# One load of 128 rows in place of loads of 112 and of six rows

## The chip, the cores and the metric

The kernel runs on one core of a Trainium2 chip. The metric is device time in microseconds (us), the median of several executions. Five engines work side by side: TensorE (PE; its weight loads are PEld), VectorE (DVE), ScalarE (ACT), GpSimd (POOL) and SyncE (SP), which here issues nearly all DMAs. Sixteen DMA engines move the data.

## The reference

A causal dynamic convolution over seven tokens feeds a soft mixture of experts, and that feeds a mixture of experts with one expert per token.

```python
# x [4, 3584, 192], weight_gen [4, 3584, 8, 7], float32
w = softmax(weight_gen, axis=-1)              # seven taps a token and head
x_pad = concat([zeros((B, 6, D)), x], axis=1)
out[b, s, h, :] = sum(w[b, s, h, k] * x_pad[b, s + k, h, :] for k in range(7))
x = out.reshape(14336, 192)
# soft MoE: logits = x @ phi (32 slots); dispatch softmax over tokens gives slot inputs,
# eight expert MLPs of four slots each, combine softmax over slots gives tokens
# second MoE: the gate's best expert of eight for each token, scaled by two gates
```

## The kernel before, in words

The convolution is done as matrix products with a banded matrix. A sequence of 3,584 tokens is cut into 32 runs of `BT` = 112 outputs. The matrix of one run and one head has 112 columns (the outputs) and `BI` = 118 rows (the inputs: six tokens in front, and the 112 themselves), with seven diagonals of taps. `band` (L316) makes it, for eight heads at once, on VectorE or GpSimd: it multiplies a tile of taps by a 0/1 mask. `conv` (L330) multiplies it with x on TensorE (L336), head by head.

A block `g` (there are `NG` = 32) holds two batches and two runs of outputs; a pair of blocks `m` holds all four batches. `load_x(g)` (L294) brings the x rows of a block into one of three buffers, `load_v(m)` (L277) the taps of a pair of blocks into one of two buffers `vt`. The taps come from `vscr` in DRAM: their softmax is made in six pieces on VectorE, GpSimd and ScalarE (L150 to L207), turned so that a diagonal becomes a column, and stored there by `w_store` (L209). `vscr` has K - 1 = 6 rows in front of each sequence, which a store of zeros fills (L596).

The 118 rows are brought by two loads for each run `q`: one of 112 rows (L305 for x, L280 for taps) and one of the last six (L307 and L282). So a block issues four x loads, and a pair of blocks four tap loads. The first run of a sequence has no tokens in front; GpSimd writes zeros there (L299).

The main loop over `g` (from L648) issues in this order: `load_x(g + 2)`, on odd blocks `load_v` two pairs ahead, the copies out of the block before, the bands of block g + 1, the convolution of block g in between, scores and the dispatch softmax of the pairs before, and at its end one load of expert weights for the soft MoE (`load_moe(g - 1)`: L268, L270 and L272, 512, 256 and 768 KB in turn, for blocks 1 to 24). All of these loads go through SyncE's one queue in the order of the program, as do the loads (L146) and stores (L212) of the tap pieces. A load of x waits until the convolution that last read its buffer is over, a load of taps until its bands are made and its `vscr` rows are stored. The order of the steps is written out by hand (`PRO`, `PS`, `CS`). After the 32 blocks come the slot MLP, the gate, and the second MoE, which writes the output; they are not touched.

Of the kernel before, what the change touches and what calls it, by code (L numbers as in the profile page):

```python
# [9 lines left out]
F32 = mybir.dt.float32  # L10
# [4 lines left out]
ALU = mybir.AluOpType  # L15
# [43 lines left out]
def dram_ap(t, off, dims):  # L59
    return bass.AP(t.tensor, t.offset + off, [list(d) for d in dims])  # L60
# [3 lines left out]
def attn_moe_moe_kernel(ctx: ExitStack, tc: tile.TileContext, x, wgen, phi, mw1, mw2, w_gate, w_ogate, w1, w2, out, dbg=None):  # L64
    nc = tc.nc
    P = 128
    B, S, D = x.shape
    H, K = wgen.shape[2], wgen.shape[3]
    GR = D // H
    HK = H * K  # L70
# [1 line left out]
    E, _, F = mw1.shape  # L72
    N = B * S
    BT = 112
    BI = BT + K - 1
    MT = 2 * BT
    NM = S // MT
    NG = 2 * NM
    RH = 28 + K - 1
    FC = F // P  # L80
    NT = N // P
    SROW = S + K - 1
    HC = D // 2
    CW = 4 * MT
    NC = S // CW
# [2 lines left out]
    xf = x.rearrange("b s d -> (b s) d")  # L88
# [6 lines left out]
    cpool = pool(ctx, "cpool", 1)  # L95
    dpool = ctx.enter_context(tc.tile_pool(name="dpool", bufs=1, space=DRAM))
    vscr = dpool.tile([B, SROW, HK], F32, tag="vscr", name="vscr")
    cscr = dpool.tile([2, NS, N], F16, tag="cscr", name="cscr")
# [30 lines left out]
    def w_load(i):  # L129
        rt, t0 = RTS[i], T0S[i]  # L130
        rh = rt + K - 1

        e = wg01[:, i * rh : (i + 1) * rh] if i < 2 else pw.tile([P, RH, H, K], F32, tag="wg", name=f"wg_{i}", bufs=2)
        ef = e.rearrange("p t h k -> p (t h k)")
        off = t0 * HK
        last = t0 + 32 * rt == S
        if last:
            nc.gpsimd.memset(ef[:, rt * HK : rh * HK], 0.0)

            for a, z in ((0, 16), (16, 31)):  # L140
                nc.sync.dma_start(
                    ef[B * a : B * z, rt * HK : rh * HK],
                    dram_ap(wf, off + (a + 1) * rt * HK, [[rt * HK, z - a], [S * HK, B], [1, (K - 1) * HK]]),
                )
        n = rt if last else rh
        nc.sync.dma_start(ef[:, 0 : n * HK], dram_ap(wf, off, [[rt * HK, 32], [S * HK, B], [1, n * HK]]))  # L146
        pcs[i] = [e, None, None, None]
# [61 lines left out]
    def w_store(i):  # L209
        rt, t0 = RTS[i], T0S[i]  # L210
        vr = pcs.pop(i)[2].rearrange("p t h k -> p (t h k)")
        nc.sync.dma_start(dram_ap(vscr, (t0 + K - 1) * HK, [[rt * HK, 32], [SROW * HK, B], [1, rt * HK]]), vr[:, 0 : rt * HK])  # L212

    wg01 = pw.tile([P, RH, H, K], F32, tag="wg", name="wg_01", bufs=2)
    w_load(0)
    zrow = cpool.tile([K - 1, HK], F32, tag="zrow", name="zrow")
    nc.gpsimd.memset(zrow, 0.0)
    w_load(1)
    warmup = cpool.tile([K - 1, 1], F32, tag="warmup", name="warmup")
    nc.scalar.activation(warmup, zrow[:, 0:1], AF.Exp)  # L220


# [1 line left out]
    make_identity(nc, ident)  # L224
    mask_s = cpool.tile([BI, BT], F32, tag="mask_s", name="mask_s")
    nc.gpsimd.memset(mask_s, 1.0)

    nc.gpsimd.affine_select(mask_s, mask_s, pattern=[[-1, BT]], compare_op=ALU.is_ge, fill=0.0, base=0, channel_multiplier=1)
    nc.gpsimd.affine_select(mask_s, mask_s, pattern=[[1, BT]], compare_op=ALU.is_ge, fill=0.0, base=K - 1, channel_multiplier=-1)
    phi_p = cpool.tile([P, 2, NS], F32, tag="phi_p", name="phi_p")  # L230
    nc.gpsimd.memset(phi_p, 0.0)
    ones1 = cpool.tile([P, P], F16, tag="ones1", name="ones1")
# [12 lines left out]
    vbank = pt.tile([P, 512], F32, tag="mask", name="vbank", bufs=1)  # L245
    mask = vbank[0:BI, 0:BT]

# [29 lines left out]
    def load_v(m):  # L277
        vt = p2.tile([BI, B, 2, HK], F32, tag="vt", name=f"vt_{m}")
        for q in range(2):
            nc.sync.dma_start(vt[0:BT, :, q, :], dram_ap(vscr, (m * MT + q * BT) * HK, [[HK, BT], [SROW * HK, B], [1, HK]]))  # L280
        for q in range(2):
            nc.sync.dma_start(vt[BT:BI, :, q, :], dram_ap(vscr, (m * MT + (q + 1) * BT) * HK, [[HK, K - 1], [SROW * HK, B], [1, HK]]))  # L282
        vts[m] = vt


# [3 lines left out]

    xbuf = [px.tile([BI, 4 * D + 8], F32, tag=f"x4{i}", name=f"x4_{i}") for i in range(3)]  # L290
    for t in xbuf:
        nc.gpsimd.memset(t[:, 4 * D : 4 * D + 8], 0.0)

    def load_x(g):  # L294
        m, hf = divmod(g, 2)
        t = xbuf[g % 3]
        if m == 0:
            for bb in range(2):
                nc.gpsimd.memset(t[0 : K - 1, 2 * bb * D : (2 * bb + 1) * D], 0.0)  # L299
        r0 = 2 * hf * S + m * MT - (K - 1)  # L300
        v = t[:, 0 : 4 * D].rearrange("p (b q d) -> p b q d", b=2, d=D)
        h = K - 1
        for q in range(2):
            a = h if m == 0 and q == 0 else 0
            nc.sync.dma_start(v[a : a + BT, :, q, :], dram_ap(xf, (r0 + q * BT + a) * D, [[D, BT], [S * D, 2], [1, D]]))  # L305
        for q in range(m == 0, 2):
            nc.sync.dma_start(v[BT:BI, :, q, :], dram_ap(xf, (r0 + (q + 1) * BT) * D, [[D, h], [S * D, 2], [1, D]]))  # L307
        xts[g] = t


# [254 lines left out]
    h = RH // 2  # L565
    for i, st in PS.items():
        ops = [
            (w_load, i), (w_max, i, 0, h), (w_max, i, h), (w_sub, i, nc.gpsimd, 0, h), (w_sub, i, nc.gpsimd, h), (w_exp, i, 0, h), (w_exp, i, h),
            (w_red, i, 0, h), (w_red, i, h), (w_add, i, 0, h), (w_add, i, h), (w_rec, i, 0, h), (w_rec, i, h), (w_rot, i, range(0, 3)), (w_rot, i, range(3, K)),
        ]  # L570
        for t, (f, *a) in zip(st, ops):
            if t >= 0:
                at_step(t, f, *a)
        at_step(st[-1], w_store, i)
# [7 lines left out]
    for g in range(3):  # L582
        load_x(g)
# [9 lines left out]
    w_rot(0, range(0, 6))  # L593
    w_rot(0, range(6, K), nc.gpsimd)
    w_store(0)
    nc.scalar.dma_start(dram_ap(vscr, 0, [[HK, K - 1], [SROW * HK, B], [1, HK]]), zrow.unsqueeze(1).to_broadcast([K - 1, B, HK]))  # L596
    load_v(0)

    def warm_up():
# [4 lines left out]
    def store_1():  # L604
        w_store(1)
        load_phi(4, H)
        load_v(1)
        w_load(3)
# [39 lines left out]
    for g in range(NG):  # L648
        m, hf = divmod(g, 2)
        run = g < NG  # L650
        if 2 < g + 2 < NG:
            load_x(g + 2)
        if run and hf == 1 and m + 2 < NM:
            load_v(m + 2)
# [97 lines left out]
    for i in range(2):  # L752
        r, v = slice(64 * i, 64 * i + 64), slice(16 * i, 16 * i + 16)
# [557 lines left out]
    for f in range(2):  # L1311
        a, z = 4 * f, 4 * f + 4
# [50 lines left out]
    for g in range(NGR):  # L1363
        hi, lo = hh.pop(g)
        ot = f2.tile([P, 4, D], F32, tag="ot", name=f"ot_{g}", bufs=3)
        for j in range(4):
            if j == HJ and g + 2 < NGR:
                hidden(Gm, g + 2, 0, 1)
            t = 4 * g + j
# [57 lines left out]
```

## Time and profile before

| | us |
|---|---|
| median of 3 executions | 281.48 |
| lowest, highest | 281.1, 283.66 |
| the profiled execution | 284.04 |
| its span, first to last instruction | 282.3 |
| TensorE, VectorE busy | 222.2, 228.4 |
| GpSimd, ScalarE busy | 151.0, 148.0 |

The profile is of one execution of its own, and its rows add up to its own span. A group of rows below says which view it is; a wait is put down to what ended it last. "PEclk" is the share of TensorE's full clock that was granted, "DMA share" the mean busy share of the 16 DMA engines.

### The profile page before, as it was taken

How to read it: one execution, taken by the hardware profiler on the slowest of the kernel's cores; microseconds unless marked ns; L12 is line 12 of the kernel's file. 1: busy time of each engine (PE TensorE's matmuls, PEld its weight loads, DVE VectorE, ACT ScalarE, POOL GpSimd, SP SyncE). 2: the span in 40 equal slices, each digit the busy share in tenths (PEclk: the TensorE clock that was granted, in tenths of full speed). 3: DMA queues.
4: the chain of work that ended last, by engine and by line, in shares of the span. 5: the costliest groups of instructions: out<-in, count | busy, mean ns of one | idle time of the engine just before them, and what ended most of it. 6: DMA issues, size and time to landing. Idle time of an engine off the chain costs nothing.

```text
span 282.3 us, 9568 instructions
## 1 busy us (share of the span) xinstructions
PE 222.2 (79%) x3844; PEld 164.2 (58%) x3844; DVE 228.4 (81%) x469; ACT 148.0 (52%) x349; POOL 151.0 (53%) x143
## 2 busy tenths in 40 slices
PE   0017299587986997998969979999878899989980
PEld 0016166365654675776647656754656688878970
DVE  2999999956699399899986998477868797788980
ACT  3102166334653366654574757735405496969970
POOL 6285698785486299658974697325401122314000
PEclk9999989998898699999999999999995999999996
DMA  6625287779699879979998963238579246578773
GB/s 208 160 61 172 92 226 207 231 225 263 177 233 278 240 190 241 262 157 242 295 233 202 228 162 106 63 80 188 128 200 243 49 147 192 179 229 266 233 229 112
DMA packets 63256, 53.82 MB, mean 191 GB/s; under 512 B 19649, under 2 KB 59685, under 8 KB 63205
## 3 DMA queue, kind: packets, MB, share of 16 engines
q1 hardware_dynamic: 63175, 53.14, 69.9%
q8 instruction: 32, 0.52, 0.9%
q14 instruction: 19, 0.16, 0.2%
q10 hardware_dynamic: 30, 0.01, 0.0%
HBM read 37.07 MB, written 16.06 MB: 188 GB/s over the span
## 4 chain that ended last, share of the span: by engine, by line
PE 43%; DVE 19%; DMA 18%; ACT 6%; issue 5%; SPq 1%; POOL 1%; ACTq 0%; DVEq 0%; POOLq 0%
DMA x<-in_x_dram 11%; PE tp L365 8%; PE psA L336 7%; DVE bt L322 5%; PE psB L336 5%; PE L L351 4%; DMA out_dram<-ot 3%; PE op L1372 3%; PE sp L430 2%; PE op L1375 2%; PE op L1374 2%; PE op L1373 2%; DMA vt<-vscr 2%; DMA w1t<-in_moe_w_dram 2%; PE hp L1064 2%
## 5 line engine op out<-in xcount | busy, mean ns | idle before, releaser
L322 POOL TENSOR_TENSOR bt<-vt,mask_s 118x896 f32<-118x896 f32 x51 | 101.5, 2015 | 39.4 <-PE psB L336 19.4
L322 DVE TENSOR_TENSOR bt<-vt,vbank 118x896 f32<-118x896 f32 x77 | 80.0, 1079 | 3.6 <-PE psB L336 2.3
L336 PE MATMUL psA<-bt,x 118*32 118x112 f32 x1024 | 53.7, 279 | 29.2 <-issue 11.2
L369 ACT ACTIVATE at<-tp 112x384 f32<-112x384 f32 x62 | 30.2, 490 | 54.2 <-PE tp L365 53.8
L336 PE MATMUL psB<-bt,x 118*32 118x112 f32 x1024 | 53.6, 272 | 0.5 <-DMA x<-in_x_dram 0.2
L336 PEld LDWEIGHTS psA<-bt,x 118*32 118x32 f32 x1024 | 25.5, 113 | 47.2 <-issue 23.9
L365 PE MATMUL tp<-ident,aT 128*112 128x128 f32 x256 | 44.1, 293 | 0.7
L365 PEld LDWEIGHTS tp<-ident,aT 128*112 128x112 f32 x256 | 26.9, 137 | 17.1 <-issue 12.8
L336 PEld LDWEIGHTS psB<-bt,x 118*32 118x32 f32 x1024 | 33.3, 116 | 1.7 <-issue 0.9
L1377 ACT ACTIVATE ot<-op,S 128x192 f32<-128x192 f32 x77 | 29.4, 437 | 5.9 <-DMA out_dram<-ot 3.1
L1372 PE MATMUL op<-wm,hi 128*128 128x192 f16 x112 | 27.5, 245 | 3.7 <-DVE ot L1379 2.0
L1375 PE MATMUL op<-Ml,cT 128*128 128x192 f16 x112 | 27.5, 246 | 0.2 <-DVE Ml L1296 0.2
L1373 PE MATMUL op<-wm,lo 128*128 128x192 f16 x112 | 27.5, 245 | 0.1
L1374 PE MATMUL op<-wm,hi 128*128 128x192 f16 x112 | 27.5, 246 | 0.1
L1066 DVE SCALAR_TENSOR_TENSOR lo<-hp,hi 128x512 f16<-128x512 f32 x28 | 19.1, 681 | 3.6 <-ACT hi L1065 3.6
L166 ACT ACTIVATE wg<-wg 128x952 f32<-128x952 f32 (+3 forms) x11 | 9.0, 828 | 21.0 <-DVE wg L162 9.1
L351 PE MATMUL L<-aT,phi_p 128*32 128x224 f32 x256 | 19.3, 395 | 0.0
L1065 ACT ACTIVATE hi<-hp 128x512 f16<-128x512 f32 x28 | 16.9, 605 | 3.6 <-PE hp L1064 3.3
L344 ACT ACTIVATE aT<-psA 128x448 f32<-128x448 f32 x31 | 16.7, 539 | 3.2 <-PE psA L336 3.2
L162 POOL TENSOR_TENSOR wg<-wg,mx 128x952 f32<-128x952 f32 (+3 forms) x9 | 14.1, 1573 | 7.2 <-DVE mx L155 7.2
L344 ACT ACTIVATE aT<-psB 128x448 f32<-128x448 f32 x31 | 17.0, 548 | 0.0
L1379 DVE TENSOR_SCALAR ot<-op,S 128x192 f32<-128x192 f32 x35 | 13.7, 410 | 3.0 <-DMA out_dram<-ot 2.9
(259 smaller groups left out, 388.4 us busy)
## 6 DMA issues: line engine op xcount, KB each, us to landing
x<-in_x_dram SPq DMA_DIRECT2D x64, 168.0 KB
w2s<-in_moe_w_dram SPq DMA_DIRECT2D x8, 768.0 KB
out_dram<-ot SPq DMA_DIRECT2D x15, 384.0 KB
w1a<-in_moe_w_dram SPq DMA_DIRECT2D x8, 512.0 KB
cT<-cscr SPq DMA_DIRECT2D x8, 448.0 KB
vt<-vscr SPq DMA_DIRECT2D x32, 98.0 KB
out_dram<-ot SPq DMA_DIRECT2D x9, 288.0 KB
vscr<-vr SPq DMA_DIRECT2D x3, 784.0 KB
```

The costliest lines, as they stand in the source:

```text
L322: (nc.gpsimd if onp else nc.vector).tensor_tensor(bt.rearrange("p h (r k) -> p h r k", k=K), vt.unsqueeze(2).to_broadcast([BI, H, BT // K, ...
L336: nc.tensor.matmul(pss[g][h // 4][r : r + 32, q, :], xt[:, q * D + GR * h : q * D + GR * h + 32], bt[:, h, :], start=True, stop=True, tile ...
L344: nc.scalar.activation(aT[:, c, :], ps.rearrange("p q t -> p (q t)"), AF.Copy)
L351: nc.tensor.matmul(Ls[m][32 * b : 32 * b + 32, :], phi_p[:, c, :], aTs[2 * m + b // 2][:, c, (b % 2) * MT : (b % 2 + 1) * MT], start=(c == ...
L365: nc.tensor.transpose(tp[:, q, c, :], aTs[g][:, c, o : o + BT], ident)
L369: nc.scalar.activation(o, i, AF.Copy)
L1066: low = lambda: nc.vector.scalar_tensor_tensor(lo[:, f, :], hp, 0.0, hi[:, f, :], op0=ALU.max, op1=ALU.subtract)
L1372: nc.tensor.matmul(op, hi[:, 0, tok], wm2[:, 0, :], start=True, stop=False)
L1373: nc.tensor.matmul(op, lo[:, 0, tok], wm2[:, 0, :], start=False, stop=False)
L1374: nc.tensor.matmul(op, hi[:, 0, tok], wm2[:, 1, :], start=False, stop=False)
L1375: nc.tensor.matmul(op, cT[:, t * P : (t + 1) * P], Ml, start=False, stop=True)
L1377: nc.scalar.activation(ot[:, j, :], op, AF.Copy, scale=S0[:, t : t + 1])
```

## The change

A run's input has 128 rows (`BI = P`): 16 tokens in front of the outputs (`PAD = P - BT`) and the 112 themselves. The mask keeps the seven diagonals, ten rows lower, and the added ten rows of the banded matrix are zeros. `vscr` gets 16 rows in front of each sequence, the store of zeros and the memsets of x cover 16 rows, and each run's rows come in one load: two loads a block for x, two a pair of blocks for the taps.

```diff
--- before.py
+++ after.py
@@ -72,14 +72,15 @@
     E, _, F = mw1.shape
     N = B * S
     BT = 112
-    BI = BT + K - 1
+    PAD = P - BT
+    BI = P
     MT = 2 * BT
     NM = S // MT
     NG = 2 * NM
     RH = 28 + K - 1
     FC = F // P
     NT = N // P
-    SROW = S + K - 1
+    SROW = S + PAD
     HC = D // 2
     CW = 4 * MT
     NC = S // CW
@@ -209,14 +210,14 @@
     def w_store(i):
         rt, t0 = RTS[i], T0S[i]
         vr = pcs.pop(i)[2].rearrange("p t h k -> p (t h k)")
-        nc.sync.dma_start(dram_ap(vscr, (t0 + K - 1) * HK, [[rt * HK, 32], [SROW * HK, B], [1, rt * HK]]), vr[:, 0 : rt * HK])
+        nc.sync.dma_start(dram_ap(vscr, (t0 + PAD) * HK, [[rt * HK, 32], [SROW * HK, B], [1, rt * HK]]), vr[:, 0 : rt * HK])
 
     wg01 = pw.tile([P, RH, H, K], F32, tag="wg", name="wg_01", bufs=2)
     w_load(0)
-    zrow = cpool.tile([K - 1, HK], F32, tag="zrow", name="zrow")
+    zrow = cpool.tile([PAD, HK], F32, tag="zrow", name="zrow")
     nc.gpsimd.memset(zrow, 0.0)
     w_load(1)
-    warmup = cpool.tile([K - 1, 1], F32, tag="warmup", name="warmup")
+    warmup = cpool.tile([PAD, 1], F32, tag="warmup", name="warmup")
     nc.scalar.activation(warmup, zrow[:, 0:1], AF.Exp)
 
 
@@ -225,8 +226,8 @@
     mask_s = cpool.tile([BI, BT], F32, tag="mask_s", name="mask_s")
     nc.gpsimd.memset(mask_s, 1.0)
 
-    nc.gpsimd.affine_select(mask_s, mask_s, pattern=[[-1, BT]], compare_op=ALU.is_ge, fill=0.0, base=0, channel_multiplier=1)
-    nc.gpsimd.affine_select(mask_s, mask_s, pattern=[[1, BT]], compare_op=ALU.is_ge, fill=0.0, base=K - 1, channel_multiplier=-1)
+    nc.gpsimd.affine_select(mask_s, mask_s, pattern=[[-1, BT]], compare_op=ALU.is_ge, fill=0.0, base=K - 1 - PAD, channel_multiplier=1)
+    nc.gpsimd.affine_select(mask_s, mask_s, pattern=[[1, BT]], compare_op=ALU.is_ge, fill=0.0, base=PAD, channel_multiplier=-1)
     phi_p = cpool.tile([P, 2, NS], F32, tag="phi_p", name="phi_p")
     nc.gpsimd.memset(phi_p, 0.0)
     ones1 = cpool.tile([P, P], F16, tag="ones1", name="ones1")
@@ -277,9 +278,7 @@
     def load_v(m):
         vt = p2.tile([BI, B, 2, HK], F32, tag="vt", name=f"vt_{m}")
         for q in range(2):
-            nc.sync.dma_start(vt[0:BT, :, q, :], dram_ap(vscr, (m * MT + q * BT) * HK, [[HK, BT], [SROW * HK, B], [1, HK]]))
-        for q in range(2):
-            nc.sync.dma_start(vt[BT:BI, :, q, :], dram_ap(vscr, (m * MT + (q + 1) * BT) * HK, [[HK, K - 1], [SROW * HK, B], [1, HK]]))
+            nc.sync.dma_start(vt[:, :, q, :], dram_ap(vscr, (m * MT + q * BT) * HK, [[HK, BI], [SROW * HK, B], [1, HK]]))
         vts[m] = vt
 
 
@@ -296,15 +295,12 @@
         t = xbuf[g % 3]
         if m == 0:
             for bb in range(2):
-                nc.gpsimd.memset(t[0 : K - 1, 2 * bb * D : (2 * bb + 1) * D], 0.0)
-        r0 = 2 * hf * S + m * MT - (K - 1)
+                nc.gpsimd.memset(t[0:PAD, 2 * bb * D : (2 * bb + 1) * D], 0.0)
+        r0 = 2 * hf * S + m * MT - PAD
         v = t[:, 0 : 4 * D].rearrange("p (b q d) -> p b q d", b=2, d=D)
-        h = K - 1
         for q in range(2):
-            a = h if m == 0 and q == 0 else 0
-            nc.sync.dma_start(v[a : a + BT, :, q, :], dram_ap(xf, (r0 + q * BT + a) * D, [[D, BT], [S * D, 2], [1, D]]))
-        for q in range(m == 0, 2):
-            nc.sync.dma_start(v[BT:BI, :, q, :], dram_ap(xf, (r0 + (q + 1) * BT) * D, [[D, h], [S * D, 2], [1, D]]))
+            a = PAD if m == 0 and q == 0 else 0
+            nc.sync.dma_start(v[a:BI, :, q, :], dram_ap(xf, (r0 + q * BT + a) * D, [[D, BI - a], [S * D, 2], [1, D]]))
         xts[g] = t
 
 
@@ -593,7 +589,7 @@
     w_rot(0, range(0, 6))
     w_rot(0, range(6, K), nc.gpsimd)
     w_store(0)
-    nc.scalar.dma_start(dram_ap(vscr, 0, [[HK, K - 1], [SROW * HK, B], [1, HK]]), zrow.unsqueeze(1).to_broadcast([K - 1, B, HK]))
+    nc.scalar.dma_start(dram_ap(vscr, 0, [[HK, PAD], [SROW * HK, B], [1, HK]]), zrow.unsqueeze(1).to_broadcast([PAD, B, HK]))
     load_v(0)
 
     def warm_up():
```

## Rows read from the trace of the kernel before

**Rows 1.** Windows: length, busy PE, PEld, DVE, ACT, POOL, PEclk, DMA share, GB/s

```profile
45.00:60.00 15.00, 11.39 (x230) 7.73 (x222) 13.90 (x27) 6.16 (x16) 11.50 (x7) 1.00 0.83 237
60.00:80.00 20.00, 17.00 (x335) 11.56 (x333) 13.71 (x19) 10.81 (x24) 13.33 (x8) 0.91 0.85 200
80.00:100.00 20.00, 16.45 (x300) 11.51 (x302) 15.48 (x31) 8.13 (x21) 11.42 (x7) 0.83 0.94 257
100.00:120.00 20.00, 17.95 (x406) 12.92 (x402) 17.92 (x25) 12.90 (x30) 17.30 (x10) 1.00 0.89 227
120.00:140.00 20.00, 18.80 (x395) 12.81 (x388) 19.79 (x38) 10.08 (x26) 15.25 (x10) 1.00 0.89 237
```

**Rows 2.** TensorE's waits, 45:100, 100:140, 140:170 us: total, times, longest

```profile
PE psA L336 <- DMA x<-in_x_dram: 7.0, 3, 2.6
...
PE psA L336 <- DMA x<-in_x_dram: 2.6, 3, 1.6
...
PE psA L336 <- DMA x<-in_x_dram: 1.4, 1, 1.4
```

**Rows 3.** Lines L307, L282: issue ns min/median/max; who waited (us, times)

```profile
L307 SPq DMA_DIRECT2D x<-in_x_dram x62: 272/290/443, 4.0 to 172.3; - x62
...
  PE psA L336: 11.0, 7
...
L282 SPq DMA_DIRECT2D vt<-vscr x32: 263/340/896, 14.8 to 168.0; - x32
...
  POOL bt L322: 8.8, 2
```

**Rows 4.** SyncE's issues in order of time from 63.8 us: start, us, issue

```profile
63.86 0.40 SPq L272 DMA_DIRECT2D w2s<-in_moe_w_dram  x1
64.35 2.28 SPq L305 DMA_DIRECT2D x<-in_x_dram  x2
66.68 0.69 SPq L307 DMA_DIRECT2D x<-in_x_dram  x2
67.98 0.85 SPq L280 DMA_DIRECT2D vt<-vscr  x2
68.88 3.24 SPq L282 DMA_DIRECT2D vt<-vscr  x2
...
72.77 0.32 SPq L305 DMA_DIRECT2D x<-in_x_dram  x1
```

**Rows 5.** Waits of SyncE's queue, 30 to 170 us: total, times, longest

```profile
SPq L282 <- DMA w2s<-in_moe_w_dram: 7.7, 4, 2.2
...
SPq L282 <- DMA wg<-in_weight_gen_dram: 4.0, 1, 4.0
SPq L282 <- DMA w1a<-in_moe_w_dram: 3.9, 4, 1.3
```

**Rows 6.** A window at 90 us; matmuls on x in it; all of L336

```profile
90.00:94.30 4.30, 4.21 (x56) 2.90 (x58) 2.69 (x3) 0.00 (x0) 0.00 (x0) 0.50 0.75 187
...
L336 PE MATMUL psA<-bt,x x16: 363/394/396, 90.1 to 91.0; 118*32 118x112 f32 x16
...
L336 PE MATMUL psA<-bt,x x1024: 256/259/397, 22.7 to 181.8; 118*32 118x112 f32 x171
```

**Rows 7.** The page's DMA packets and main queue

```profile
DMA packets 63256, 53.82 MB, mean 191 GB/s; under 512 B 19649, under 2 KB 59685, under 8 KB 63205
...
q1 hardware_dynamic: 63175, 53.14, 69.9%
```

**Rows 8.** Matmuls of L430 and L351; two groups of VectorE

```profile
L430 PE MATMUL sp<-at,d x256: 324/327/352, 48.3 to 186.7; 112*32 112x193 f32 x128
...
L351 PE MATMUL L<-aT,phi_p x256: 350/353/581, 36.7 to 183.3; 128*32 128x224 f32 x128
...
L322 DVE TENSOR_TENSOR bt<-vt,vbank 118x896 f32<-118x896 f32 x77 | 80.0, 1079 | 3.6 <-PE psB L336 2.3 <-DMA vt<-vscr 0.7
...
L513 DVE TENSOR_REDUCE cmx<-T 128x28 f32<-128x896 f32 x4 | 4.3, 1079 | 0.2
```

## The prediction

> **What bounds the kernel now.** I read the windows first, then TensorE's waits, then who issued what those waits were for. The change touches loads and tiles of the attention stage alone (convolution, scores and slot sums of 32 blocks, matmuls from 22.7 to 181.8 us of the span [rows 6]).
>
> In the windows [rows 1] no single engine is full between 45 and 100 us: TensorE is busy 44.8 of 55 us, VectorE 43.1, and the DMA engines run at 0.83, 0.85 and 0.94. From 100 to 140 us VectorE is nearly full (17.92 and 19.79 of 20 us). So until 100 us something makes three busy parties wait for each other, and after it VectorE sets the pace.
>
> TensorE's own waits name it [rows 2]. From 45 us on it stands 7.0 us for x until 100 us, 2.6 us until 140 and 1.4 us until 170: 11.0 us. The reader should note which x load these are. The view of the six-row load [rows 3] lists these seven waits, 11.0 us, under L307: that is the last of a block's loads to be issued, and the last to land. The six-row tap load L282 in the same way holds GpSimd for 8.8 us.
>
> Why are these late? SyncE's queue shows it [rows 4]. It issues in program order. From the w2s load at 63.86 us count on: two and two x loads, two tap loads, then the two six-row tap loads, which take 3.24 us together though one issue is 0.34 us at the median [rows 3]. The second is the eighth DMA after w2s, and the waits of the queue [rows 5] say that L282 stood for a landing of w2s 7.7 us in four waits, for wg 4.0 us, for w1a 3.9 us. So eight DMAs may be under way, each new one takes the place of the one eight before it, and in this order the second L282 always takes the place of a big weight load. Behind it stand a weight load and the next block's x load (72.77 us), and meanwhile the DMA engines run dry.
>
> **The change, part by part.** *Fewer issues.* 62 six-row x loads (0.290 us at the median) and 32 tap loads (0.340 us) go: 18.0 + 10.9 = 28.9 us of SyncE's time [rows 3].
>
> *The order of eight.* Two blocks now issue 14 DMAs (4 + 4 of x, 2 + 2 of taps, 2 of weights); after it 8 (4, 2, 2). Each DMA then takes the place of its own counterpart two blocks earlier, unless a load or store of the tap weights lies between. A pair of blocks lasts 10 us on the mean (159 us for 16), and the w2s load above landed some 8 us after its issue, so the stands of rows 5, 15.6 us, should end or shrink to the slowest landings. What is late next: an x load still waits until its buffer is free (the convolution of three blocks before), which leaves it two blocks' time, and for the tap store that waits on VectorE.
>
> *What of TensorE's wait that frees.* Three things cap it, by stage. From 45 to 100 us: the waits are 7.0 us; VectorE's idle time 55 - 43.1 = 11.9 us; the DMA engines' idle time 0.17 x 15 + 0.15 x 20 + 0.06 x 20 = 6.75 us. DMA is the tightest. Less the added traffic of this stretch (1.3 us, below) it leaves 5.5 us. From 100 to 140 us VectorE has 2.3 us idle against 2.6 us of waits; as it already sets the pace there, I take 1.0. From 140 to 170 us the one wait of 1.4 us follows the same kind of stand; I take 1.0. Sum 7.5 us.
>
> *TensorE's clock.* It was granted 0.91 and 0.83 in the windows from 60 to 100 us [rows 1], which at the half level of 1.2 GHz is (0.09 + 0.17) x 20 / 0.5 = 10.4 us. In the stretch from 90.0 us, right behind a 2.6 us wait [rows 2], it was 0.50 [rows 6], and a convolution matmul took 394 ns there against 259. If the waits go, so may these, for up to 10.4 x (1 - 259 / 394) = 3.6 us. The sum is capped by DMA, so I leave this out and keep it for the low end.
>
> *Added traffic.* A block's x rows go from 472 packets of 768 B to 512 (the first two blocks: 20 more each), the taps of a pair of blocks from 944 of 224 B to 1,024: 1,240 + 1,280 packets and 40 of the zero store, 1.25 MB. The queue's row [rows 7] gives 0.699 x 16 x 282.3 = 3,157 us of engine time for 53.14 MB in 63,175 packets: 59.4 us a MB, 50 ns a packet. By bytes the added packets cost 74 us of engine time, 4.6 us on 16 engines; by count 128 us, 8.0 us. They are smaller than the mean of 841 B, so bytes are nearer: 4.6 us over 32 blocks, 1.3 us over the nine that fall between 45 and 100 us. Both figures assume an even spread before. It is not even: of the 19,649 packets under 512 B the code's own rows explain 15,104 + 24 + 384 + 192; 3,945 are left for 308 DMAs, and with 16 closing packets for each there would be 4,928, with 16 for 214 and 6 for 94 there are 3,988. So a six-row load runs on about six engines, which then already carry 8 rows for the others' 7. If those six set the landing, the added traffic costs 0; that is the other end of its range.
>
> The Trainium skill has the rule behind this (DMA: Bandwidth & Descriptors, section on why a DMA increments its semaphore by 16): the number of engines is the largest up to 16 that divides the slowest dimension, on the lowest-numbered ones. The packet count agrees. By it the 1.3 us would be 0, and the sum 8.8 us.
>
> *The engines.* 128 rows in place of 118 in matmuls and taps. Matmul time follows columns: 112 columns 259 ns [rows 6], 193 with 112 rows 327, 224 with 128 rows 353 [rows 8]; that is 0.84 ns a column each time, so 10 rows cost nothing. VectorE's tap product (118 x 896) takes 1,079 ns, its maximum over 128 x 896 too [rows 8]: 0. GpSimd's product is the one form without such a pair. Ten rows in 118 would be 8% if it went by rows, and with 8% more its fullest window [rows 1] would go from 17.30 to 18.7 of 20 us, still short of full. Masks and memsets of 16 rows come once, ahead of the first taps, and the zero store (16 rows for 6) lies beside VectorE's softmax chain of the start; at most tenths of a us. No wait is added: each tap product and convolution waits for one load in place of two.
>
> **The sum.** The profiled execution took 284.04 us (span 282.3), 0.9% over the median of 281.48. 284.04 - 7.5 = 276.5; carried to the median, 281.48 - 7.5 = 274.0 us.
>
> **Rivals.** *B, the DMA engines are the bound, not the queue.* Then requests issued earlier only lie longer behind weight loads, land as before, and the time is 281.5, give or take 1.5. For it: shares of 0.83 to 0.94, and every x wait ends with a landing. Against: the stands of rows 5, with idle engines behind them. The Trainium skill speaks for it (same page, section on issuing engines): it calls the time that a sequencer takes to initiate a DMA usually small beside the DMA. The rows agree for the issue alone; the stand behind a slot is another matter.
>
> *C, slower.* The same bound, and the added rows go on the path: in stretches where the share is full, each added packet delays the x load behind it. Price 4.6 us by bytes (8.0 by count): 286 us. It decides if the share reaches 0.97 or more from 45 to 160 us and TensorE's x waits grow past 11 us. Against it: the busiest six engines get nothing more.
>
> *D, more.* All 11.0 us of waits go, and the clock's 3.6 us: 266.9 us. It needs VectorE to use its idle time in full and DMA to fill its own.
>
> *E, the order of eight doesn't change* because the places are given out in another way than I read: 281.
>
> **Chances.** Forecast 0.55 (its own range 270 to 278.5: from the added traffic at zero and half the clock's gain, to half of the sum gone to VectorE), B 0.19, C 0.08, D 0.15, E 0.03. The range of 268 to 282.5 us leaves out C and about half of D. A measurement of this kernel tells about 1% from no change, so faster means under 278.7: nearly all of the forecast, and D: 0.70. Same: B, E and the forecast's upper end, 0.22. Slower: 0.08.
>
> **What would show it.** Right: L282's stands on weight loads gone; TensorE's x waits from 45 us on below 4 us; DMA's share from 45 to 100 us at 0.93 or more; next in the list of TensorE's waits the taps of VectorE. The tail from the slot MLP on keeps its length of about 100 us. Wrong: stands of the same length under another line; x issued earlier and landing no earlier; VectorE's idle time unchanged while x waits fall, which would mean that its own chain (tap softmax, stores) is what x waited beside.

## The result, and the profile after

| | before | after |
|---|---|---|
| median, us (lowest to highest) | 281.67 (281.1 to 283.66, one run more than above) | 273.43 (272.12 to 275.21) |
| the profiled execution | 284.04 | 272.13 |
| its span | 282.3 | 270.4 |

The ratio is 0.9699, with a 95% interval of 0.9613 to 0.9785: 8.2 us less, against 7.5 us forecast. The two profiled executions lie 11.9 us apart, since the one before is a slow run, 2.4 us above its kernel's median, and the one after lies 1.3 us below its own; so a difference of two profiles tells here where time went, the medians how much.

The windows of the kernel after, with the columns of [rows 1]:

```profile
45.00:60.00 15.00, 12.89 (x279) 8.81 (x281) 14.30 (x29) 7.65 (x20) 13.38 (x7) 1.00 0.90 260
60.00:80.00 20.00, 18.82 (x394) 12.57 (x386) 18.93 (x29) 12.17 (x28) 16.37 (x11) 1.00 1.04 295
80.00:100.00 20.00, 17.93 (x396) 12.71 (x399) 18.85 (x30) 12.79 (x29) 16.55 (x9) 1.00 0.99 265
100.00:120.00 20.00, 19.92 (x429) 13.93 (x425) 19.05 (x35) 11.34 (x29) 15.12 (x10) 1.00 1.02 274
120.00:140.00 20.00, 15.83 (x308) 10.89 (x300) 18.56 (x28) 8.91 (x22) 13.26 (x7) 0.83 0.78 226
```

From 45 to 100 us everything is fuller than in [rows 1]: TensorE 49.6 us against 44.8, VectorE 52.1 against 43.1, the DMA share 0.90 to 1.04, the clock at 1.00. (The share adds up the times of packets and, as the 1.04 shows, can pass 1.) From 120 to 140 us the reverse: TensorE falls from 18.80 to 15.83 us. These are two findings, and the prediction has only the first.

TensorE's waits from 45 to 100 us, and behind "..." from 100 to 140 us; from 140 to 170 us there are none:

```profile
PE psA L332 <- DVE bt L318: 3.4, 4, 1.6
PE psA L332 <- DMA x<-in_x_dram: 1.1, 2, 0.6
...
PE tl L405 <- ACT at L365: 4.1, 1, 4.1
```

The waits for x were 11.0 us in [rows 2] and are 1.1. VectorE's taps come first now, and one wait of 4.1 us is new.

The waits of SyncE's queue, 30 to 170 us (L303 is now the one line of x loads, L281 of tap loads, L213 the tap store):

```profile
SPq L303 <- PE psB L332: 27.0, 23, 4.6
SPq L213 <- DVE vr L208: 19.7, 4, 8.8
...
SPq L281 <- DMA vscr<-vr: 4.2, 3, 1.8
SPq L273 <- DMA w1a<-in_moe_w_dram: 2.7, 3, 1.7
```

The tap load's 15.6 us behind w2s, wg and w1a [rows 5] are gone; 2.7 us on w1a are left, under the w2s load (L273), which in the order of the program is again the eighth DMA behind it. The queue now stands for buffers (the x load waits until a convolution has read its buffer) and for the tap store that waits on VectorE, the two that the prediction named as next. The same place in the order of time as [rows 4]:

```profile
58.37 0.37 SPq L273 DMA_DIRECT2D w2s<-in_moe_w_dram  x1
58.85 1.07 SPq L303 DMA_DIRECT2D x<-in_x_dram  x2
60.02 1.60 SPq L281 DMA_DIRECT2D vt<-vscr  x2
61.68 1.46 SPq L269 DMA_DIRECT2D w1a<-in_moe_w_dram  x1
63.24 1.70 SPq L303 DMA_DIRECT2D x<-in_x_dram  x2
```

The next block's x load is issued 4.9 us behind w2s; before it was 8.9 us (63.86 to 72.77).

How far the convolution got is seen in its matmuls alone, 64 to a block. Kernel before, L336, then kernel after, L332: window, its length, matmuls busy and their count, weight loads, clock, DMA share, GB/s:

```profile
45.00:100.00 55.00, 22.78 (x612) 15.28 (x608) 0.91 0.88 231
100.00:140.00 40.00, 20.42 (x568) 13.57 (x564) 1.00 0.89 232
```

```profile
45.00:100.00 55.00, 26.58 (x768) 17.95 (x768) 1.00 0.98 274
100.00:140.00 40.00, 18.67 (x513) 12.66 (x512) 0.91 0.90 250
```

The 612 matmuls that took 55 us take 55 x 612 / 768 = 43.8 us at the new pace: 11 us less in this stretch. The first matmul of single blocks, read from the same view in order of time, gives 9.4: block 5 starts at 47.5 us in place of 50.0, block 17 at 103.5 in place of 115.4. In the next stretch the changed kernel does fewer (513 for 568). The last convolution matmul starts at 170.5 us against 181.8 [rows 6].

What the change adds, on the page and in the views of the two lines:

```profile
DMA packets 65261, 55.06 MB, mean 204 GB/s; under 512 B 20415, under 2 KB 61691, under 8 KB 65211
...
q1 hardware_dynamic: 65131, 54.37, 72.1%
```

```profile
L332 PE MATMUL psA<-bt,x x1024: 256/259/397, 20.9 to 170.5; 128*32 128x112 f32 x171
...
L318 DVE TENSOR_TENSOR bt<-vt,vbank x77: 1050/1081/1108, 19.7 to 166.0; 128x896 f32<-128x896 f32 x77
L318 POOL TENSOR_TENSOR bt<-vt,mask_s x51: 1950/2012/2611, 17.1 to 163.4; 128x896 f32<-128x896 f32 x51
```

Ten more rows cost the engines nothing: 259 ns a matmul as in [rows 6], 1,081 ns a tap product on VectorE against 1,079 [rows 8], and on GpSimd 2,012 ns against 2,004 (medians). The main queue moves 1.23 MB more than in [rows 7], and its time on the engines goes down, 0.721 x 16 x 270.4 = 3,119 us for 3,157.

### The profile page after: what moved, and what is told of

It is laid out like the page before. It is cut to its first block, busy times and chain, and to the rows that moved or that the text cites. A ratio compares the mean times of both kernels' runs of the same rounds, so it can differ in the third digit from the quotient of the medians.

```text
span 270.4 us, 9410 instructions
## 1 busy us (share of the span) xinstructions
PE 221.1 (82%) x3844; PEld 163.0 (60%) x3844; DVE 230.0 (85%) x469; ACT 147.8 (55%) x349; POOL 151.2 (56%) x143
## 4 chain that ended last, share of the span: by engine, by line
PE 42%; DVE 29%; DMA 9%; ACT 7%; issue 5%; SPq 1%; ACTq 0%; DVEq 0%
PE tp L361 8%; DVE bt L318 8%; PE psA L332 7%; PE psB L332 5%; DVE vr L208 5%; PE L L347 5%; DMA out_dram<-ot 4%; DMA x<-in_x_dram 3%; PE op L1368 2%; PE sp L426 2%; DVE vbank L188 2%; PE op L1371 2%; DMA w1t<-in_moe_w_dram 2%; PE op L1370 2%; PE op L1369 2%
## 5 line engine op out<-in xcount | busy, mean ns | idle before, releaser
L318 POOL TENSOR_TENSOR bt<-vt,mask_s 128x896 f32<-128x896 f32 x51 | 101.7, 2021 | 17.0 <-PE psB L332 11.0
L318 DVE TENSOR_TENSOR bt<-vt,vbank 128x896 f32<-128x896 f32 x77 | 80.0, 1081 | 1.2 <-DMA vt<-vscr 0.5
L332 PE MATMUL psA<-bt,x 128*32 128x112 f32 x1024 | 53.2, 278 | 15.1 <-issue 9.4
L332 PE MATMUL psB<-bt,x 128*32 128x112 f32 x1024 | 51.6, 270 | 0.4 <-issue 0.4
L332 PEld LDWEIGHTS psA<-bt,x 128*32 128x32 f32 x1024 | 25.2, 113 | 32.5 <-issue 20.5
L332 PEld LDWEIGHTS psB<-bt,x 128*32 128x32 f32 x1024 | 31.6, 115 | 1.0 <-issue 0.6
L1062 DVE SCALAR_TENSOR_TENSOR lo<-hp,hi 128x512 f16<-128x512 f32 x28 | 19.1, 682 | 2.9 <-ACT hi L1061 2.9
L347 PE MATMUL L<-aT,phi_p 128*32 128x224 f32 x256 | 20.3, 385 | 0.0
L167 ACT ACTIVATE wg<-wg 128x952 f32<-128x952 f32 (+3 forms) x11 | 9.0, 828 | 19.1 <-DVE wg L163 9.1
```

The source lines that it names most:

```text
L318: (nc.gpsimd if onp else nc.vector).tensor_tensor(bt.rearrange("p h (r k) -> p h r k", k=K), vt.unsqueeze(2).to_broadcast([BI, H, BT // K, ...
L332: nc.tensor.matmul(pss[g][h // 4][r : r + 32, q, :], xt[:, q * D + GR * h : q * D + GR * h + 32], bt[:, h, :], start=True, stop=True, tile ...
L347: nc.tensor.matmul(Ls[m][32 * b : 32 * b + 32, :], phi_p[:, c, :], aTs[2 * m + b // 2][:, c, (b % 2) * MT : (b % 2 + 1) * MT], start=(c == ...
L1062: low = lambda: nc.vector.scalar_tensor_tensor(lo[:, f, :], hp, 0.0, hi[:, f, :], op0=ALU.max, op1=ALU.subtract)
```

## The experiments

Three theories stood at first. *Places*: the order of the eight DMAs under way and fewer issues made the gain. *Rows* (below also *shape*, the number of rows in a load): loads of 128 rows are cheaper for the DMA engines, and the order matters little. *Collision*: the new 4.1 us wait is a VectorE step held up by GpSimd, an accident of the new timing. Below, "us a MB" is engine time of the main queue, its share x 16 x span over its MB: 59.4 before, 57.4 after. Each ratio is to runs of the kernel before that were taken beside the experiment; runs taken together are a set.

**split16.** The kernel after, with each run in a load of 112 rows and one of the last 16: the added rows, without the merge. dt and dx stand for the DRAM patterns, whose rows go with the slices.

```diff
-            nc.sync.dma_start(vt[:, :, q, :], dt)
+            nc.sync.dma_start(vt[0:BT, :, q, :], dt)
+        for q in range(2):
+            nc.sync.dma_start(vt[BT:BI, :, q, :], dt)
...
-            nc.sync.dma_start(v[a:BI, :, q, :], dx)
+            nc.sync.dma_start(v[a:BT, :, q, :], dx)
+        for q in range(2):
+            nc.sync.dma_start(v[BT:BI, :, q, :], dx)
```

> The layout after the change (128 rows), but every run's rows again in two loads, of 112 and of 16 rows, both of which divide among 16 engines: 14 DMAs for a pair of blocks, as before. Queue theory (the eight places and SyncE's issues were the cause): 279 to 284 us, second tap loads stand for weight loads again, TensorE's x waits about 9 to 12 us. Rows theory (what helped is that no six-row load lands late on a few engines): 272 to 276 us, x waits below 4 us.

Measured: 287.66 us, ratio to before 1.0261 (1.0138 to 1.0383). TensorE's and SyncE's waits of this kernel, 45 to 170 and 30 to 170 us:

```profile
PE psA L336 <- DMA x<-in_x_dram: 19.7, 11, 4.7
...
SPq L283 <- DMA w2s<-in_moe_w_dram: 7.8, 4, 2.3
SPq L283 <- DMA w1a<-in_moe_w_dram: 3.1, 4, 1.1
```

The second tap load (L283) stands behind the same weight loads as in [rows 5], and x waits grow to 19.7 us. Fourteen DMAs and more rows are slower than the kernel before, at 60.1 us a MB, and slower than either theory had it. The added rows without the merge are a loss; what part of it comes from second loads of 16 rows, with 16 closing packets in place of six, isn't told apart.

**one118.** The kernel before, with its 118 rows in one load: the new number of DMAs, without the added rows (`vt[:, :, q, :]` and `v[a:BI, :, q, :]` over 118 rows).

> The layout before (118 rows), each run in one load: 8 DMAs for a pair of blocks, as after the change. If only the number of DMAs counts: 272 to 276 us. If a load of 118 rows runs on two engines (118 = 2 x 59), a block's two x loads put 236 packets of 768 B on each of two engines, 10 us at 43 ns, and a pair's taps 472 of 224 B, 9 us: about 30 us a pair of blocks in place of 10, so 450 to 620 us.

Measured: 536.91 us, ratio 1.9199 (1.8988 to 1.9411). The page's packets, and a window from 100 to 200 us:

```profile
DMA packets 61375, 53.81 MB, mean 101 GB/s; under 512 B 17769, under 2 KB 57805, under 8 KB 61325
```

```profile
100.00:200.00 100.00, 49.01 (x698) 32.20 (x698) 30.11 (x49) 21.65 (x50) 23.57 (x13) 0.69 0.28 84
```

The time is within the range for two engines; the 43 ns a packet in that estimate stand in no row here. The packets under 512 B tell on how many engines a load runs. They are 1,880 fewer than in [rows 7], which is 94 x (16 + 6 - 2): each pair of loads closed with 16 and six packets, the single load closes with two. The DMA share is 0.28 at 84 GB/s, and TensorE is busy 49 of 100 us. The Trainium skill (DMA: Bandwidth & Descriptors, section on why a DMA increments its semaphore by 16) has the rule, the largest number up to 16 that divides the rows, so two for 118; the counts agree. So with 118 rows the merge is a loss.

**dummy.** The kernel after, with a load of 64 bytes in each place from which a load was taken (94 of them, into a tile that nothing reads): the order of before, the shape of after.

```diff
+    def tiny():
+        i = next(junks)
+        nc.sync.dma_start(junk[:, i : i + 1], dram_ap(xf, i, [[D, 16], [1, 1]]))
...
+        for q in range(2):
+            tiny()              # load_v, after its two loads
...
+        for q in range(m == 0, 2):
+            tiny()              # load_x, after its two loads
```

> The kernel after the change, with a tiny load (16 rows of 4 bytes into a tile that nobody reads) in each place where a six-row load was issued: 14 DMAs a pair of blocks, but no bytes and nobody waiting for the tiny ones. Queue theory: most of the gain is lost, 278 to 283 us, and SyncE stands at tiny loads for weight loads. Rows theory: 272 to 275 us.

Measured: 279.4 us, ratio 0.998 (0.9932 to 1.0029), x waits again:

```profile
PE psA L343 <- DMA x<-in_x_dram: 11.5, 5, 4.2
...
SPq L281 <- DMA w2s<-in_moe_w_dram: 4.5, 6, 1.1
```

The tiny loads (L281) now stand for w2s. Their own packets are not the loss: the main queue's engine time is 3,098 us (0.697 x 16 x 277.8), below the 3,119 after, and 57.0 us a MB. So the good shape alone, without the places, gives nothing back: the places (order and number of issues together) are needed.

**x_only** and **taps_only.** One of the two merges alone, the other in the form of split16.

> The layout after the change with one load a run for x, while the taps come in loads of 112 and of 16 rows: 10 DMAs a pair of blocks. Queue theory: between, nearer to the kernel after than the one with both split (287.7 us): 274 to 280 us, TensorE's x waits below 5 us. If the taps' loads were what held the queue (SyncE stood at them): 282 us or more.

> The layout after the change with one load a run for the taps, while x comes in loads of 112 and of 16 rows: 12 DMAs a pair of blocks. Queue theory: 279 to 286 us, stands for weight loads under the lines of x in place of the taps' line, x waits of 6 us or more. If the taps' loads held the queue: 274 to 278 us.

Measured: x_only 270.19 us, 0.965 (0.9582 to 0.9717); taps_only 278.25 us, 0.991 (0.9858 to 0.9962). The merge of x carries the gain; x_only was expected at 274 to 280, so the merge of the taps was taken to be worth more than it is. With ten DMAs a pair of blocks the gain is as large as with eight: it isn't needed that each DMA takes the place of its own counterpart. taps_only falls between its two ranges; x waits are 4.8 us, and the two x loads stand for w2s 4.3 and 3.8 us, at 60.0 us a MB (x_only: 58.0).

**rows120.** The kernel after with eight rows in front (`PAD = 8`, `BI = BT + PAD`): the same eight DMAs in the same order, fewer bytes.

> The kernel after the change with 120 rows (8 in front) in one load in place of 128 rows, 8 DMAs a pair of blocks as before it. 120 rows divide among 15 engines, 8 rows each, as 128 do among 16. If the added rows cost by the busiest engine: no change, 272 to 275 us. If they cost by bytes (about 1 MB less, 3.8 us of 16 engines at 59.4 us a MB): 269 to 272 us.

Measured: 280.31 us, 0.9996 (0.9956 to 1.0037), above both ranges. Its packets, its windows at 60 and 100 us, and two of TensorE's waits from 45 to 170 us:

```profile
DMA packets 63111, 54.06 MB, mean 196 GB/s; under 512 B 19257, under 2 KB 59541, under 8 KB 63061
```

```profile
60.00:80.00 20.00, 18.18 (x378) 12.32 (x377) 18.51 (x28) 11.52 (x27) 15.59 (x10) 1.00 1.01 235
...
100.00:120.00 20.00, 19.32 (x421) 13.44 (x414) 18.52 (x26) 13.32 (x31) 14.70 (x8) 1.00 1.05 236
```

```profile
PE tl L405 <- ACT at L365: 4.1, 1, 4.1
...
PE psB L332 <- DMA x<-in_x_dram: 0.3, 2, 0.2
```

At the same share the DMA engines move 235 and 236 GB/s, where those of the kernel after move 295 and 274: 61.3 us a MB. The small packets are 1,158 fewer than after: 1,024 + 32 tap and zero rows, 8 for the zero store's engines, and 94, one for each load, which makes 15 engines. The places did end the x waits (0.3 us), and still the time is that of the kernel before: a wait that is gone is not yet time that is gained. As it stands this kernel gains nothing. But the 4.1 us wait of the kernel after is in it too, so the places alone are not judged before that wait is away (rows120_sel, below).

**sel_early** and **before_sel.** On VectorE's list three sums of 128 x 32 and a copy (`sel`, `sel4`) stand in block 20. Here they stand ahead of the first `w_max`, in the kernel after and in the one before.

```diff
+    nc.vector.tensor_tensor(sel, ident[:, 0:32], ident[:, 32:64], op=ALU.add)
+    nc.vector.tensor_tensor(sel, sel, ident[:, 64:96], op=ALU.add)
+    nc.vector.tensor_tensor(sel, sel, ident[:, 96:128], op=ALU.add)
+    nc.vector.tensor_copy(sel4, sel.unsqueeze(1).to_broadcast([P, 4, NS]))
     w_max(0)
```

The reason is this stretch of the kernel after in order of time (start, us, engine, line):

```profile
119.78 5.87 POOL L318 TENSOR_TENSOR bt<-vt,mask_s 128x896 f32<-128x896 f32 x3
121.18 0.65 DVE L700 TENSOR_TENSOR sel<-ident 128x32 f32<-128x32 f32 x1
121.87 1.92 DVE L701 TENSOR_TENSOR sel<-sel,ident 128x32 f32<-128x32 f32 x1
123.82 1.88 DVE L702 TENSOR_TENSOR sel<-sel,ident 128x32 f32<-128x32 f32 x1
...
127.36 0.68 PE L405 MATMUL tl<-ident,dT 128*112 128x128 f32 x2 [4.08 <-ACT at L365]
```

and the same in the kernel before:

```profile
128.25 4.01 POOL L322 TENSOR_TENSOR bt<-vt,mask_s 118x896 f32<-118x896 f32 x2
...
133.16 0.18 DVE L704 TENSOR_TENSOR sel<-ident 128x32 f32<-128x32 f32 x1
133.38 0.19 DVE L705 TENSOR_TENSOR sel<-sel,ident 128x32 f32<-128x32 f32 x1
133.60 0.19 DVE L706 TENSOR_TENSOR sel<-sel,ident 128x32 f32<-128x32 f32 x1
```

Before, the sums fell between two of GpSimd's tap products and took 0.2 us each. After, they fell on a row of three and took 0.65, 1.92 and 1.88 us; VectorE's next maximum came that much later, and TensorE stood 4.1 us. Right behind it the clock was low (0.83 in the window from 120 us).

> The kernel after the change, with the four VectorE steps that make sel and sel4 (used only at the end) moved from block 20 to the first microseconds. In the profile after the change three of them take 0.65, 1.92 and 1.88 us while GpSimd makes taps, against 0.18 to 0.19 us before, and TensorE then waits 4.1 us and runs at half clock for a while. If VectorE stands because GpSimd runs: the wait and the half-clock stretch go, 266 to 270 us. If the wait has another cause that is next late: 272 to 275 us.

> The kernel before, with the VectorE steps for sel and sel4 moved to the first microseconds. In the profile before they took 0.18 to 0.19 us, with GpSimd idle beside them. If the gain of that move after the change came from VectorE standing beside GpSimd: no change here, 279 to 282 us. If the move is worth something in itself: 274 to 277 us.

Measured: sel_early 265.99 us, 0.9538 (0.9424 to 0.9652), the lowest median of all; before_sel 280.18 us, 0.9985 (0.9944 to 1.0027), as the collision theory had both. The convolution of sel_early, 100 to 140 us:

```profile
100.00:140.00 40.00, 21.00 (x604) 14.23 (x608) 1.00 0.96 268
```

604 matmuls for 513, at a full clock: the 513 would take 6.0 us less at this pace. By the medians the move is worth 5.0 to 7.4 us in the changed kernel (against 271.03 and 273.43, from other sets), by the ratios to each set's own kernel before 0.6 to 1.6%, or 1.7 to 4.5 us; in the kernel before it is worth nothing. The traces tell which kernels have the collision: two of the three sums take 1.9 us each in after, after_again, x_only and rows120, and 0.19 us in before, split16, dummy and taps_only.

**collide.** The kernel after with one sum (`ident` + `ident`) and one product (`ident` x 2.0) of 128 x 32 in every block on VectorE, behind its bands; nothing reads them. It was to show whether two operands in SBUF are what is held.

> The kernel after the change with two added small VectorE steps in each block from block 1 on, right behind its band: a sum of two 128 x 32 pieces of SBUF into SBUF, and one 128 x 32 piece of SBUF times a constant. Alone they take about 0.2 us. If VectorE stands beside GpSimd's taps only when it reads two operands from SBUF: the sum has a median well over 0.2 us and a maximum of 1.9 us or more, the product stays below 0.4 us. If both stand, or neither, the longest are alike. The time grows by 10 to 30 us under the first theory.

Measured in one execution: 298.36 us, 27 above after_again. Of 30 each the sums took 185 ns at the median and up to 2,004, the products 172 and up to 2,027. Two of each kind, beside GpSimd:

```profile
98.10 1.99 POOL L319 TENSOR_TENSOR bt<-vt,mask_s 128x896 f32<-128x896 f32 x1
98.14 2.00 DVE L675 TENSOR_TENSOR junk<-ident 128x32 f32<-128x32 f32 x1
100.07 0.17 DVE L676 TENSOR_SCALAR junk<-ident 128x32 f32<-128x32 f32 x1
...
106.97 3.91 POOL L319 TENSOR_TENSOR bt<-vt,mask_s 128x896 f32<-128x896 f32 x2
106.99 2.00 DVE L676 TENSOR_SCALAR junk<-ident 128x32 f32<-128x32 f32 x1
```

A step that starts just behind a GpSimd product ends with it; one in the gap at 100.07 us takes 0.17 us. The steps took 22.4 and 21.9 us in all, where at their medians they would take 5.6 and 5.2. The collision is real, but my version of it, that only steps with two operands in SBUF are held, falls: the product has one. VectorE's tap products, with the mask in PSUM, stay at 1,075 ns and are not held.

**rows120_sel, x_only_sel, after_again.** The two kernels above with `sel` early, and the kernel after once more, in one set.

> 120 rows in one load (8 DMAs a pair of blocks), with sel and sel4 made at the start, so that no collision on VectorE hides what the loads do. Places theory (the eight places are the whole gain): 265 to 269 us, as with 128 rows. Shape theory (loads of 128 rows also take less DMA-engine time a MB, 57.4 against 61.3 us): 272 to 276 us, between the kernel before (281) and 128 rows (266).

> x in one load of 128 rows a run, taps in loads of 112 and 16 rows, and sel and sel4 made at the start. If the taps' merge is worth nothing once x is merged: 264 to 267 us. If the 270.2 us of x_only was a lucky meeting of VectorE and GpSimd: 267 to 271 us.

> The kernel after the change once more, beside the others on the same chip: 272 to 275 us.

Measured: rows120_sel 275.28 us, 0.9691 (0.9581 to 0.9801); x_only_sel 267.16 us, 0.9485 (0.941 to 0.956); after_again 271.03 us, 0.9598 (0.95 to 0.9696), a little below its range. In x_only and in rows120 too `sel` early is a gain, from 0.965 and 1.000. With the collision gone, the places alone do gain: rows120_sel is 3.1% below the kernel before. And 120 rows cost 8.1 us more than x_only_sel, which issues ten DMAs a pair of blocks in place of eight. x_only_sel and sel_early can't be told apart, so the merge of the taps, on top of that of x, is worth nothing that shows here.

| places in the queue | 128-row loads | kernel | ratio to before | without the collision |
|---|---|---|---|---|
| 14 a pair | no | before | 1 | 0.9985 (before_sel) |
| 14 a pair | no, added rows | split16 | 1.026 | the same, has none |
| 14 a pair | yes | dummy | 0.998 | the same, has none |
| 12 a pair | taps alone | taps_only | 0.991 | the same, has none |
| 10 a pair | x alone | x_only | 0.965 | 0.9485 (x_only_sel) |
| 8 a pair | no (120 rows) | rows120 | 1.000 | 0.969 (rows120_sel) |
| 8 a pair | yes | after, after_again | 0.970, 0.960 | 0.954 (sel_early) |

The last column is the answer to the first two theories: the shape alone gives nothing, the places alone 3%, both together 4.6%. From the first to the last convolution matmul of each profile, which leaves out that the stage starts at different times, the order is the same: before 159.1 us, dummy 157.2, rows120_sel 152.3, x_only_sel 147.1, sel_early 144.8.

## Why the prediction was right, and where it was not

**What bounds the kernel.** The reading held: the stands of L282 went, x waits fell to 1.1 us (forecast: below 4), the DMA share from 45 to 100 us is 0.98 (0.93 or more), VectorE's taps are next. dummy shows the cause by putting the places back: 11.5 us of x waits and 279.4 us. E, an order of eight that doesn't change, falls with the stands.

**The term of 5.5 us, 45 to 100 us,** was too small by the profiles: 9.4 to 11 us came. Up to 3.7 of these may be spread between executions (2.4 and 1.3 us, above), so the excess is somewhere between nothing and 4 us. The step that failed is the cap by the DMA engines' idle time of 6.75 us. It took three things as fixed. What they move in a busy microsecond rose, from 231 GB/s at a share of 0.88 to 274 at 0.98, 262 to 280 GB/s a full share. The share is no bound at 1: it reached 1.04. And the traffic of the stretch doesn't have to fall in it; before 45 us, with the same number of convolution matmuls, more had already been moved (views of L336 and L332 again, 180 GB/s for 161):

```profile
0.00:45.00 45.00, 11.99 (x284) 8.83 (x288) 0.96 0.57 161
...
0.00:45.00 45.00, 12.13 (x288) 8.92 (x288) 0.96 0.63 180
```

With the waits the low clock of this stretch went too (0.91 to 1.00), for which the prediction had counted up to 3.6 us and left them out on the strength of the same cap.

**The added traffic** had the wrong sign in the changed kernel. By bytes 4.6 us were expected, with 0 as the other end; engine time fell by 38 us. The runs show two parts: the added rows with second loads of 16 do cost (split16 is 7.0 us above the kernel before in the same set, between the 4.6 and the 8.0), and loads of 128 rows cost less a MB (57.0 in dummy and 57.4, against 60.0 to 60.1 with x in 112 and 16 rows). The six engines that I read out of the packet count are confirmed by its change, 766 more: 1,280 + 40 rows, 10 for the zero store's engines, less 94 x 6 for the loads removed. That they set the landing isn't shown: split16 has no six-row load, and is slower.

**The terms of 1.0 and 1.0 us behind 100 us** failed. The x waits went as forecast, but from block 17 (11.9 us ahead) to the last matmul (11.3 ahead) 0.6 us were lost, not 2.0 won. The cause is the collision of `sel` with GpSimd, which sel_early takes away (604 matmuls for 513 from 100 to 140 us). The prediction had "no wait is added", which is right for the code and wrong for the schedule. A smaller one of this kind helped: convolution starts at 20.9 us in place of 22.7. Two VectorE steps run at 17 us, where GpSimd begins its first three tap products: one of the tap rotation (L207 before), which takes 0.89 or 1.98 us, and a subtraction of 128 x 672 (L162), which takes 0.84 or 2.6 to 2.7 us. In the traces convolution starts at 22.7 us where both are long (before, rows120_sel), at 20.9 where one is (after, dummy, before_sel, rows120) and at 19.1 where neither is (sel_early, x_only, split16, taps_only). That this is the same collision is argued from the lengths; no run took it away. It comes and goes in kernels with and without the change, so these 1.8 us are not shown to be an effect of it.

**The engines' cost of nought** for ten more rows held, on GpSimd too.

**So 274.0 for 273.43** is a right mechanism with errors of both signs, and that the two lie so close is luck. By the two profiles the gain is 2.5 us up to block 5, 9.4 up to block 17, -0.6 up to the last convolution matmul and 0.6 in the tail (forecast: nought; 100.5 to 99.9 us from that matmul to the end): 11.9 us. The medians give 8.2 and, in the repeat, 11.1. Against 7.5 the first stage was undersized, by up to 4 us, the luckier start was not counted, and the loss behind it was not seen. D (266.9 us: all waits and the clock's part) is about what the change gives when the collision is away: 265.99 and, for x_only_sel, 267.16. B falls, since a queue that issues earlier did end the waits. C's price and its x waits are met in split16, without the merge (287.66 us for 286, 19.7 us for more than 11), but not its mechanism: the DMA share there was 0.89 from 45 to 160 us, not the 0.97 that C asks for.

What stays open is why a 128-row load costs less a MB than 112 and 16 rows, which by the packet counts run on 16 engines too (x_only has 512 small packets more than the kernel after, 16 for each of its 32 added loads), and why 15 engines cost 61.3. How crowded the engines are doesn't explain it: with 128 rows it is 57.1 us at a share of 0.654 (collide) and 57.2 at 0.739 (sel_early). Of the gain without the collision the places alone make 3.1% and the shape, on top of them, 1.5 to 2.1%; in one set the second step is the 8.1 us between rows120_sel and x_only_sel, of which up to 3.7 can be the accident of the start (convolution begins at 22.7 and 19.0 us in their profiles), so its size is uncertain. Order and number of issues are not parted by any run, nor is it shown what sets the number eight, the chip or the way the program is built.

## What to carry to other kernels

Read a queue's waits by what they stand for: a small load that always takes the place of a big one is late however small it is, and leaving it out can be worth more than the bytes that this adds. Then look at the time and not at the wait alone: in rows120 the waits went and the time stayed. Before loads are merged, look at the number of rows: 118 in one load nearly doubled the time, 120 gave nothing as it stood (3% with the sums moved), 128 gave 3 to 4%. When a stage gets faster, look behind it for steps that now meet others: by the medians 5 to 7 us, by the ratios 2 to 5, of some 13 to 15 that this change could give were lost to three sums of 0.2 us each.

## What was not expected of the hardware

VectorE steps of 128 x 32 fp32, 0.17 to 0.19 us alone, last up to 2.0 us when a GpSimd product with operands in SBUF (2.0 us) has just begun; a sum of two SBUF operands and a product of one by a constant alike, while products with an operand in PSUM kept their 1.08 us. The Trainium skill (SBUF — State Buffer, section on who interferes with whom) states that the two engines share a pair of ports, held by whoever starts first for its whole instruction, by VectorE for two SBUF inputs and for forms such as a product with a constant that can run in a two-port mode. collide agrees on both (2,004 and 2,027 ns).

Loads in 128 rows cost 57.0 to 57.4 us of engine time a MB, x in 112 and 16 rows 60.0 to 60.1, in 120 rows 61.3 to 61.7, in 118 rows on two engines 55.5 (one118), with packets of the same 768 and 224 bytes.
